# Attention with a hashed mask, then a mixture of experts: the routing's work of a batch on other steps

## The chip, the cores and the metric

The kernel runs on one core of one Trainium2 chip. The time is what the device takes for one execution, in microseconds (us). TensorE (PE, with its weight loads PEld), VectorE (DVE), ScalarE (ACT), GpSimd (POOL) and the DMA queues run side by side, each through its own instructions in order, and wait for each other by semaphores.

## The reference, cut to what matters

Four batches of eight heads attend over 768 positions. A key counts only if its hash bucket (six sign bits of a projection) is the query's. The result, 3072 tokens of 512 values, goes through a mixture of eight experts, of which each token takes the one with the greatest logit.

```python
def _attn_ref(q, k, v, proj):            # (4, 8, 768, 64)
    mask = q_bucket[:, :, :, None] == k_bucket[:, :, None, :]
    scores = np.where(mask, scale * np.matmul(q, k.transpose(0, 1, 3, 2)), -1000000000.0)
    scores = scores - np.max(scores, axis=-1, keepdims=True)
    attn = np.exp(scores)
    attn = attn / (np.sum(attn, axis=-1, keepdims=True) + 1e-09)
    return np.matmul(attn, v)

def _moe_ref(x, w_gate, w_output_gate, w1, w2):    # x (3072, 512)
    logits = x @ w_gate
    e_idx = np.argmax(logits, axis=1)
    ...
    gate_w = probs[np.arange(N), e_idx]
    eom = 1.0 / (1.0 + np.exp(-(x @ w_output_gate)))
    for e in range(E):
        mask = e_idx == e
        h = np.maximum(x[mask] @ w1[e], 0.0)
        out[mask] = gate_w[mask, None] * eom[mask, e, None] * (h @ w2[e])
```

## The kernel before

**The attention loop.** Its unit is a step: one block of 128 queries of one head. Sixteen pairs of heads of twelve steps each make 192 steps, and steps run in groups of two. In step s PE makes the scores (`scores`, L530, into one of two `ps_s` buffers), DVE takes them out with the row minimum (L534, tile `sc`), ACT exponentiates with the row sum (L542), DVE inverts the sums of two steps (L549, L550, tile `rsum`) and POOL multiplies both tiles by them (`normal`, L552), at the start of the group after. Four steps behind its scores a tile is transposed on PE (L563) and copied by ACT to `pts` (L564); behind each group PE multiplies `pts` by the values (L574, into `ps_a`). For the next pair of heads POOL and DVE split the inputs into a rounded part and a rest (L488, L496), PE projects to hash bits (L407, taken out by L410), and SP's DMA queue spreads the parts over the partitions (L505 to L513). A finished pair is copied out (L577, `ot`), transposed in blocks (L586, `xb`) and written to `x_dram` (L593).

**The routing of a batch.** When the four pairs of a batch are done, `routing(b)` makes functions that are put on steps of the batch after. Numbers n count from the start of that batch (step 48(b+1)). `logits` and `tokens` multiply by the gates' weights and turn the result to tokens. `best` finds the maximum and the exponentials. `choose` (L644 to L651) makes the one-hot choice `oneh` and its bf16 copy `ohb`. `gates` (L655 to L663) makes a token's factor. `prefix` (L668 to L673) counts on PE, from `ohb`, how many tokens before it took the same expert; `ranks` (L678 to L683) reads that out and adds to the running `base`. `cols` makes place and columns of the table (`table_cols` L198 to L205, `table_rhs` L211, L215), `hot` the one-hot of the place (L220); `table` sums them on PE (L226) and `entries` adds the sum to `tacc_e` (L229).

**What follows the third batch.** Three batches are routed within the loop; the fourth behind it. At step `late`, behind the third batch's `entries`, `pick` takes the expert with most tokens and loads its number into a register on SP. `early_gather` gathers two blocks of 128 of its tokens from `x_dram` (POOL's queue, L254), `early_turn` transposes them on PE (L266), `early_load` and `early_w1` load the expert's first weights in four pieces and split them on POOL (L175, L178). Behind the loop, the first layer of this expert runs in eight blocks (`fill`) between the fourth batch's routing, and its second weights (w2) are split on POOL.

**What sets the order.** PE, DVE, ACT and POOL run in the order in which the code is written: `plan(step, fn)` puts a function behind that step's own work, and functions of one step run in the order of their planning. The SP queue's order is made by the scheduler. Scratch tiles of the routing have one buffer each (`gp`), as has the PSUM tile `ps_m`.

Of the kernel before, what the change touches and what calls it, by code (L numbers as in the profile page):

```python
# [8 lines left out]
F32 = mybir.dt.float32  # L9
# [10 lines left out]
B, H, S, D = 4, 8, 768, 64  # L20
NB = 6
P = 128
NT = S // P
# [36 lines left out]
def lsh_attention_then_moe(  # L60
# [307 lines left out]
    with ExitStack() as actx:  # L368
# [16 lines left out]
        def plan(step, *fns):  # L385
            at.setdefault(step, []).extend(fns)
# [209 lines left out]
        def routing(b):  # L596
# [56 lines left out]
            def gates():  # L653
                den = gp.tile([P, NT], F32, name="den")
                nc.vector.tensor_reduce(den, st["ex"], AX.X, ALU.add)  # L655
                nc.vector.tensor_tensor(st["en"], st["en"], oh, ALU.mult)
                es = gp.tile([P, NT], F32, name="es")
                nc.vector.tensor_reduce(es, st["en"], AX.X, ALU.add)
                nc.vector.tensor_scalar(den, den, 1e-9, None, ALU.add)
                nc.vector.tensor_scalar(es, es, 1.0, None, ALU.add)  # L660
                nc.vector.reciprocal(den, den)
                nc.vector.reciprocal(es, es)
                nc.vector.tensor_tensor(gate[:, ts], den, es, ALU.mult)  # L663

# [19 lines left out]

            def cols():
                st["oa"], st["pos"] = table_cols(gp, rank[:, ts], NT)
                st["rhs"] = table_rhs(gp, st["oa"], oh, gate[:, ts], toki[:, ts], NT)
# [8 lines left out]
            def entries():  # L696
# [3 lines left out]
                       gates=gates, prefix=prefix, ranks=ranks, cols=cols, hot=hot, table=table, entries=entries)  # L700
# [23 lines left out]
        for b in range(B - 1):  # L724
            r = routing(b)
            for n, fn in ((6, lambda r=r: r["logits"](0, H // 2)), (8, lambda r=r: r["tokens"](0, H // 2)),
                          (10, lambda r=r: r["logits"](1, H // 2)), (12, lambda r=r: r["tokens"](1, H // 2)),
                          (13, r["best"]), (14, r["choose"]), (15, r["gates"]), (16, r["prefix"]), (16, r["ranks"]),
                          (17, r["cols"]), (18, r["hot"]), (20, r["table"]), (20, r["entries"])):
                plan(12 * (H // 2) * (b + 1) + n, fn)  # L730
# [10 lines left out]
        late = 12 * (H // 2) * (B - 1) + 21  # L741
# [77 lines left out]
        for a in range(EARLY):  # L819
            plan(late + 7 + 2 * a, lambda a=a: early_turn(a))  # L820
# [288 lines left out]
```

## Time and profile before

| | |
|---|---|
| median of 3 runs (lowest to highest) | 802.83 us (800.34 to 803.43) |
| the profiled execution, and its span | 799.08 us, 797.4 us |
| PE busy | 772.7 us (97%) |
| DVE busy | 472.4 us (59%) |
| ACT busy | 458.4 us (57%) |
| POOL busy | 383.4 us (48%) |
| DMA, mean rate | 124 GB/s |

The attention loop takes the first 466 us or so of the span, the experts the rest. A busy time is a share over all stages: it says that PE is the engine to watch, and not where it waits. A row of the order of time shows a group of like instructions: start, length, engine, line, operation, tile written and tiles read, shapes, count; in brackets, how long the engine sat idle ahead of it and whose work ended that. Several rows of an engine may overlap a little, since the next instruction starts before the last has drained; the time that one holds its engine is the difference of starts.

### The profile page before, as it was taken

Reading aid. Unit: us, or ns where it says so; the run is one execution under the profiler, and the core shown is the slowest. Engines: PE = TensorE matmul, PEld = TensorE weight load, DVE = VectorE, ACT = ScalarE, POOL = GpSimd, SP = SyncE. Lnnn points to the kernel's source line nnn. Section 1 sums busy time; section 2 is a strip of 40 time slices with the busy share of each in tenths; the row PEclk is TensorE's granted clock in tenths of the full one; section 3 lists DMA queues with packets and bytes.
Section 4 is the critical chain, followed back from the end, with each engine's and each line's share of the span. In section 5 each row is a group of like instructions: output and inputs, shape, how many; then the busy total and the mean of one; then the engine's idle time right before and its main releaser. Section 6 shows DMA issues by size and latency. Waiting matters only on the chain. (4 is left out here: it accounts for less than half of the span.)

```text
span 797.4 us, 13687 instructions
## 1 busy us (share of the span) xinstructions
PE 772.7 (97%) x4674; PEld 606.8 (76%) x4674; DVE 472.4 (59%) x1034; ACT 458.4 (57%) x934; POOL 383.4 (48%) x422
## 2 busy tenths in 40 slices
PE   7999999989999999999999999999999999999997
PEld 4776776666776667676567758888999999988895
DVE  5776666776766867666877537236363635464540
ACT  5877787667777677777677751234152534443331
POOL 6556544335444344543466773273627363745201
PEclk7999999999999999999999999999999999999999
DMA  4553554464464454565374422373444444535501
GB/s 159 127 148 74 113 128 85 104 159 83 105 150 92 98 126 87 125 142 138 63 205 102 119 65 43 120 236 126 143 146 147 154 147 150 171 127 194 198 24 38
DMA packets 84799, 98.88 MB, mean 124 GB/s; under 512 B 57999, under 2 KB 59439, under 8 KB 84720
## 3 DMA queue, kind: packets, MB, share of 16 engines
q1 hardware_dynamic: 79376, 84.58, 40.8%
q0 software_dynamic: 5200, 13.31, 5.1%
q8 instruction: 39, 0.64, 0.3%
q14 instruction: 40, 0.33, 0.1%
q10 hardware_dynamic: 144, 0.02, 0.0%
HBM read 59.49 MB, written 13.11 MB: 91 GB/s over the span
## 5 line engine op out<-in xcount | busy, mean ns | idle before, releaser
L552 POOL TENSOR_SCALAR sc<-sc,rsum 128x768 f32<-128x768 f32 x192 | 180.4, 953 | 224.2 <-DVE rsum L550 116.1
L534 DVE TENSOR_SCALAR_CACHE_REDUCE sc<-ps_s 128x768 f32<-128x768 f32 x192 | 183.2, 956 | 110.7 <-PE ps_s L530 103.6
L564 ACT COPY pts<-ps_t 128x384 f32<-128x384 f32 x384 | 164.2, 481 | 92.3 <-PE ps_t L563 91.8
L542 ACT ACTIVATE sc<-sc,mn 128x768 f32<-128x768 f32 x192 | 181.3, 944 | 28.7 <-DVE sc L534 19.5
L563 PE MATMUL ps_t<-ident,sc 128*128 128x128 f32 x1152 | 158.4, 273 | 6.6 <-POOL sc L552 3.6
L563 PEld LDWEIGHTS ps_t<-ident,sc 128*128 128x128 f32 x1152 | 135.9, 140 | 19.9 <-issue 7.0
L574 PE MATMUL ps_a<-pts,vt 128*64 128x384 f32 x768 | 144.8, 499 | 0.0
L530 PE MATMUL ps_s<-xr,xl 128*128 128x384 f32 x384 | 118.0, 389 | 4.6 <-DVE sc L534 4.5
L530 PEld LDWEIGHTS ps_s<-xr,xl 128*128 128x128 f32 x384 | 58.4, 192 | 75.5 <-issue 31.8
L530 PE MATMUL ps_s<-yr,yl 76*128 76x384 f32 x384 | 101.2, 344 | 1.7 <-POOL yr L439 1.6
L312 PE MATMUL ps_s<-xh,w1h 128*128 128x256 f32 (+7 forms) x288 | 97.7, 339 | 2.8 <-DVE hl L323 2.0
L323 DVE SCALAR_TENSOR_TENSOR hl<-ps_s,hh 128x256 fp32r<-128x256 f32 (+8 forms) x40 | 34.0, 849 | 111.7 <-ACT hh L322 111.7
L312 PE MATMUL ps_s<-xlo,w1h 128*128 128x256 f32 (+7 forms) x288 | 95.9, 333 | 0.0
L312 PE MATMUL ps_s<-xh,w1l 128*128 128x256 f32 (+7 forms) x288 | 95.8, 333 | 0.0
L286 POOL DMA_INDIRECT xq<-x_dram,idx x75 | 83.0, 1107 | 21.6 <-issue 21.3
L329 POOL DMA_INDIRECT out_dram<-yo,sid x29 | 31.4, 1084 | 116.0 <-ACT yo L328 61.8
L574 PEld LDWEIGHTS ps_a<-pts,vt 128*64 128x64 f32 x768 | 46.7, 136 | 50.5 <-issue 48.7
L322 ACT ACTIVATE hh<-ps_s 128x256 fp32r<-128x256 f32 (+8 forms) x40 | 29.1, 727 | 94.6 <-PE ps_s L312 94.6
L530 PEld LDWEIGHTS ps_s<-yr,yl 76*128 76x128 f32 x384 | 71.0, 192 | 2.4 <-POOL yr L439 2.4
L312 PEld LDWEIGHTS ps_s<-xh,w1h 128*128 128x128 f32 x288 | 54.7, 190 | 5.8 <-DVE hl L323 2.5
L312 PEld LDWEIGHTS ps_s<-xh,w1l 128*128 128x128 f32 x288 | 54.7, 190 | 1.1
L312 PEld LDWEIGHTS ps_s<-xlo,w1h 128*128 128x128 f32 x288 | 54.6, 189 | 1.2
(204 smaller groups left out, 1008.1 us busy)
## 6 DMA issues: line engine op xcount, KB each, us to landing
w_raw<-in_w_dram SPq DMA_DIRECT2D x36, 512.0 KB
qk<-in_qkT_dram SPq DMA_DIRECT2D x32, 384.0 KB
xh<-in_w_dram SPq DMA_DIRECT2D x14, 512.0 KB
xlo<-in_w_dram SPq DMA_DIRECT2D x14, 512.0 KB
vt<-in_v_dram SPq DMA_DIRECT2D x16, 384.0 KB
xr<-xl SPq DMA_DIRECT2D x30, 192.0 KB
yr<-xl SPq DMA_DIRECT2D x30, 192.0 KB
xr<-yl SPq DMA_DIRECT2D x30, 192.0 KB
```

Of the source, the lines that this page charges most:

```text
L286: nc.gpsimd.indirect_dma_start(out=xq[:, k * P:(k + 1) * P], out_offset=None, in_=x_dram.rearrange("n (a f) -> (n a) f", a=NB32), in_offse ...
L312: nc.tensor.matmul(ps, l, r, start=first and k == 0, stop=last and k == len(pairs) - 1)
L322: nc.scalar.activation(hh, ph, AF.Relu)
L323: return lambda: nc.vector.scalar_tensor_tensor(hl, ph, 0.0, f32(hh), ALU.max, ALU.subtract)
L329: nc.gpsimd.indirect_dma_start(out=out[:, :], out_offset=bass.IndirectOffsetOnAxis(ap=sid[0:n, r, a:a + 1], axis=0), in_=yo[0:n], in_offse ...
L530: nc.tensor.matmul(ss[:, n, 0:HS], l[0:k, qs], r[0:k, n * HS:(n + 1) * HS], start=first, stop=not first)
L534: nc.vector.tensor_scalar(sc, ss[:, :, 0:HS], MASKED, None, ALU.min, ALU.min, accum_out=mn)
L542: nc.scalar.activation(pr, pr, AF.Exp, bias=mn, scale=-1.0, accum_out=sums[s // GROUP][:, k:k + 1])
L552: nc.gpsimd.tensor_scalar(live[s0 + k], live[s0 + k], rs[:, k:k + 1], 0.0, ALU.mult, ALU.add)
L563: nc.tensor.transpose(tr[:, c], pr[:, (3 * h + c) * P:(3 * h + c + 1) * P], ident)
L564: nc.scalar.copy(pts[:, 3 * h:3 * h + 3, t * P:(t + 1) * P], tr)
L574: nc.tensor.matmul(st["av"][j * D:(j + 1) * D], st["v"][:, j, c], blocks[hb][j][:, c], start=(c == 0), stop=(c == NT - 1))
```

## The change

The functions of `routing` are cut finer. `gates` becomes `gate_sums` (the two sums and the product with the choice) and `gate_values` (the five small operations on them), `cols` becomes `places` and `columns`. `gates` and `cols` themselves remain for the fourth batch, which is routed behind the loop as before. No operation is added or taken away.

For the other three batches the steps are new: choice 14 to 19, prefix and ranks 16 to 20, the gates 15 to 21 and 22, places and columns 17 to 22 and 24, the one-hot 18 to 25, the table 20 to 28 and its addition 20 to 29. Step 24 is the first of the next pair of heads. `late` moves from 21 to 29 steps into the last batch's loop, and with it all that follows the third batch; only the turns of the gathered tokens are planned one step closer to it.

```diff
-            def gates():
-                den = gp.tile([P, NT], F32, name="den")
+            def gate_sums():
+                st["den"] = den = gp.tile([P, NT], F32, name="den")
                 nc.vector.tensor_reduce(den, st["ex"], AX.X, ALU.add)
                 nc.vector.tensor_tensor(st["en"], st["en"], oh, ALU.mult)
-                es = gp.tile([P, NT], F32, name="es")
+                st["es"] = es = gp.tile([P, NT], F32, name="es")
                 nc.vector.tensor_reduce(es, st["en"], AX.X, ALU.add)
+
+            def gate_values():
+                den, es = st["den"], st["es"]
                 nc.vector.tensor_scalar(den, den, 1e-9, None, ALU.add)
...
-            def cols():
+            def places():
                 st["oa"], st["pos"] = table_cols(gp, rank[:, ts], NT)
+
+            def columns():
                 st["rhs"] = table_rhs(gp, st["oa"], oh, gate[:, ts], toki[:, ts], NT)
...
-                          (13, r["best"]), (14, r["choose"]), (15, r["gates"]), (16, r["prefix"]), (16, r["ranks"]),
-                          (17, r["cols"]), (18, r["hot"]), (20, r["table"]), (20, r["entries"])):
+                          (13, r["best"]), (19, r["choose"]), (20, r["prefix"]), (20, r["ranks"]),
+                          (21, r["gate_sums"]), (22, r["gate_values"]), (22, r["places"]), (24, r["columns"]),
+                          (25, r["hot"]), (28, r["table"]), (29, r["entries"])):
                 plan(12 * (H // 2) * (b + 1) + n, fn)
...
-        late = 12 * (H // 2) * (B - 1) + 21
+        late = 12 * (H // 2) * (B - 1) + 29
...
         for a in range(EARLY):
-            plan(late + 7 + 2 * a, lambda a=a: early_turn(a))
+            plan(late + 6 + 2 * a, lambda a=a: early_turn(a))
```

The line numbers of the changed kernel are higher: by 7 from `gate_sums` on, by 15 behind the routing.

On DVE, in the batch that follows batch 0, this stood in a row before, from the projection's bits of step 14 (`bt`) on: the choice, the scores' minimum of step 15, a split of the next pair's inputs, and the gates.

```order
L410 TENSOR_SCALAR bt<-ps_m,pj 128x384
L644 TENSOR_SCALAR eq<-df 128x48
L645 TENSOR_TENSOR eq<-eq,expi 128x48
L647 TENSOR_REDUCE ei<-eq 128x6
L648 TENSOR_TENSOR oneh<-ei,expi 128x48
L651 CAST ohb<-oneh 128x48
L534 TENSOR_SCALAR sc,mn<-ps_s 128x768
L496 SCALAR_TENSOR_TENSOR yl<-qk,pj,xl 128x384
L655 TENSOR_REDUCE den<-ex 128x6
L656 TENSOR_TENSOR en<-en,oneh 128x48
L658 TENSOR_REDUCE es<-en 128x6
L659 TENSOR_SCALAR den<-den 128x6
```

The five rows of the choice stood between the minima of steps 14 and 15, and the gates directly behind step 15's.

On DVE in the changed kernel, from the last split of that pair (step 18) on, to the first rows of the ranks of step 20:

```order
L496 SCALAR_TENSOR_TENSOR yl<-qk,pj,xl 128x384
L534 TENSOR_SCALAR sc,mn<-ps_s 128x768
L644 TENSOR_SCALAR eq<-df 128x48
L645 TENSOR_TENSOR eq<-eq,expi 128x48
L647 TENSOR_REDUCE ei<-eq 128x6
L648 TENSOR_TENSOR oneh<-ei,expi 128x48
L651 CAST ohb<-oneh 128x48
L534 TENSOR_SCALAR sc,mn<-ps_s 128x768
L549 TENSOR_SCALAR rsum<-rsum 128x2
L550 RECIPROCAL rsum<-rsum 128x2
L685 TENSOR_TENSOR off<-ps_m,base 128x48
L686 TENSOR_TENSOR off<-off,oneh 128x48
```

The choice now comes after the splits, between the minima of steps 19 and 20, and the ranks behind step 20's row sums.

On POOL at the end of the loop before, from the rest of the third piece of w1 on to the first of w2 (`x10` are five pairs of normalisations):

```order
L178 TENSOR_TENSOR w1l<-w_raw,w1h 128x1024
L552 TENSOR_SCALAR sc<-sc,rsum 128x768 x2
L175 TENSOR_SCALAR w1h<-w_raw 128x1024
L178 TENSOR_TENSOR w1l<-w_raw,w1h 128x1024
L552 TENSOR_SCALAR sc<-sc,rsum 128x768 x10
L175 TENSOR_SCALAR w2h<-w_raw 128x1024
```

And the same place of the changed kernel:

```order
L178 TENSOR_TENSOR w1l<-w_raw,w1h 128x1024
L552 TENSOR_SCALAR sc<-sc,rsum 128x768 x2
L175 TENSOR_SCALAR w1h<-w_raw 128x1024
L178 TENSOR_TENSOR w1l<-w_raw,w1h 128x1024
L552 TENSOR_SCALAR sc<-sc,rsum 128x768 x2
L175 TENSOR_SCALAR w2h<-w_raw 128x1024
```

One pair of normalisations, the loop's last, now stands behind the fourth piece where five did.

## Rows read from the trace of the kernel before

**Rows 1.** Windows: length, busy PE, PEld, DVE, ACT, POOL, clock, DMA share, GB/s.

```profile
159.17:165.54 6.37, 4.87 (x30) 3.05 (x28) 6.13 (x21) 3.17 (x9) 1.64 (x2) 1.00 0.53 124
165.54:172.45 6.91, 5.92 (x42) 4.45 (x41) 4.53 (x11) 5.78 (x14) 4.56 (x4) 1.00 0.40 84
190.85:195.20 4.35, 4.35 (x30) 3.16 (x28) 3.11 (x8) 3.51 (x9) 1.98 (x3) 1.00 0.40 85
195.20:199.56 4.36, 4.36 (x30) 3.18 (x28) 2.18 (x6) 3.46 (x9) 1.89 (x3) 1.00 0.81 167
199.56:203.94 4.38, 4.38 (x30) 3.16 (x28) 3.23 (x8) 3.43 (x9) 1.81 (x3) 1.00 0.45 119
```

**Rows 2.** Order of time, PE, where the first batch's routing ends.

```profile
161.75 0.62 PE L530 MATMUL ps_s<-xr,xl 128*128 128x384 f32 x2 [0.90 <-DVE sc L534]
...
167.50 0.87 PE L563 MATMUL ps_t<-ident,sc 128*128 128x128 f32 x6 [0.98 <-POOL sc L552]
168.22 1.48 PE L226 MATMUL ps_m<-t_rhs,t_ob 128*128 128x96 f32 x12
169.47 0.59 PE L530 MATMUL ps_s<-xr,xl 128*128 128x384 f32 x2
```

**Rows 3.** Order of time, DVE, the first batch's routing.

```profile
152.09 0.41 DVE L644 TENSOR_SCALAR eq<-df 128x48 f32<-128x48 f32 x1
...
154.42 0.96 DVE L534 TENSOR_SCALAR_CACHE_REDUCE sc<-ps_s 128x768 f32<-128x768 f32 x1
...
155.83 0.19 DVE L655 TENSOR_REDUCE den<-ex 128x6 f32<-128x48 f32 x1
...
156.93 0.55 DVE L577 COPY ot<-ps_a 128x384 f32<-128x384 f32 x1
...
159.06 0.20 DVE L678 TENSOR_TENSOR off<-ps_m,base 128x48 f32<-128x48 f32 x1
...
160.74 0.94 DVE L534 TENSOR_SCALAR_CACHE_REDUCE sc<-ps_s 128x768 f32<-128x768 f32 x1
...
162.61 0.18 DVE L198 TENSOR_TENSOR t_ge<-rank,chki 128x30 f32<-128x30 f32 x1
...
163.21 0.35 DVE L211 TENSOR_TENSOR t_rhs<-oneh,t_oa 128x192 f32<-128x192 f32 x1
...
164.14 0.95 DVE L534 TENSOR_SCALAR_CACHE_REDUCE sc<-ps_s 128x768 f32<-128x768 f32 x1
...
165.81 0.95 DVE L220 TENSOR_TENSOR t_ob<-posi,t_pos 128x768 f32<-128x768 f32 x1
```

**Rows 4.** Order of time, DVE, the odd step's minimum in a quiet window.

```profile
193.56 0.95 DVE L534 TENSOR_SCALAR_CACHE_REDUCE sc<-ps_s 128x768 f32<-128x768 f32 x1
```

**Rows 5.** The tile of gathered tokens (xg), its eight gathers' DMAs.

```profile
DMA to landing us min/median/max: 3.2/3.8/9.6
```

**Rows 6.** Order of time, POOL, the last pairs of heads and the loop's end.

```profile
428.43 1.06 POOL L175 TENSOR_SCALAR w1h<-w_raw 128x1024 fp32r<-128x1024 f32 x1
429.57 2.39 POOL L178 TENSOR_TENSOR w1l<-w_raw,w1h 128x1024 fp32r<-128x1024 f32 x1
432.38 1.79 POOL L552 TENSOR_SCALAR sc<-sc,rsum 128x768 f32<-128x768 f32 x2 [0.42 <-ACT pts L564]
...
459.08 1.80 POOL L552 TENSOR_SCALAR sc<-sc,rsum 128x768 f32<-128x768 f32 x2 [2.85 <-PE ps_s L530]
...
466.95 1.79 POOL L552 TENSOR_SCALAR sc<-sc,rsum 128x768 f32<-128x768 f32 x2 [1.72 <-PE ps_t L563]
```

**Rows 7.** Order of time, PE, the transposes of step 194.

```profile
469.66 0.88 PE L563 MATMUL ps_t<-ident,sc 128*128 128x128 f32 x6
```

**Rows 8.** Order of time, DVE, beside a piece of w1 on POOL.

```profile
430.55 1.43 DVE L549 TENSOR_SCALAR rsum<-rsum 128x2 f32<-128x2 f32 x1
```

**Rows 9.** Order of time, PE, among the experts.

```profile
732.68 0.49 PE L312 MATMUL ps_s<-xh,w1h 128*128 128x368 f32 x1 [1.99 <-DVE hl L323]
```

**Rows 10.** Windows, the stretch behind that wait.

```profile
732.90:736.30 3.40, 3.40 (x12) 3.40 (x12) 3.40 (x4) 3.21 (x4) 1.00 (x1) 0.50 0.49 129
```

More of the change, by code (lines that the diff above doesn't have):

```diff
@@ L663, in gates @@
                 nc.vector.tensor_tensor(gate[:, ts], den, es, ALU.mult)
+            def gates():
+                gate_sums()
+                gate_values()
             def prefix():
@@ L683, in ranks @@
                 nc.vector.tensor_tensor(base, base, tot, ALU.add)
+            def places():
+                st["oa"], st["pos"] = table_cols(gp, rank[:, ts], NT)
+            def columns():
+                st["rhs"] = table_rhs(gp, st["oa"], oh, gate[:, ts], toki[:, ts], NT)
             def cols():
-                st["oa"], st["pos"] = table_cols(gp, rank[:, ts], NT)
-                st["rhs"] = table_rhs(gp, st["oa"], oh, gate[:, ts], toki[:, ts], NT)
+                places()
+                columns()
             def hot():
@@ L699, in routing @@
             fns = dict(logits=logits, tokens=tokens, add_pair=add_pair, best=best, choose=choose,
-                       gates=gates, prefix=prefix, ranks=ranks, cols=cols, hot=hot, table=table, entries=entries)
+                       gates=gates, prefix=prefix, ranks=ranks, cols=cols, hot=hot, table=table, entries=entries,
+                       gate_sums=gate_sums, gate_values=gate_values, places=places, columns=columns)
             return fns
```

## The prediction, made before the changed kernel ran

> **What bounds the kernel now.** I read the granted clock first, then the engines' busy time over pairs of steps, then the order of time on TensorE, VectorE and GpSimd around a batch's routing, and last the end of the attention loop. In the windows of [rows 1] look at PE's busy time against the length of the window: a quiet pair of steps is 4.35 us long and PE is busy for all of it, at full clock. So TensorE sets the pace of the loop, and what another engine does costs nothing while it fits beneath PE. The two windows in which a batch's routing ends are longer, 6.37 and 6.91 us, and PE is busy for only 4.87 and 5.92 of them [rows 1]. What does PE wait for there? In [rows 2] scores wait 0.90 us for a score buffer that VectorE has not emptied (sc L534), and a transpose waits 0.98 us for a normalised tile (sc L552), which hangs on VectorE's row sums. VectorE is busy for 6.13 of 6.37 us there [rows 1]: the bound in this stretch is VectorE's queue, not TensorE. The three batches that are routed inside the loop show the same two lengths within 0.02 us; the fourth is routed behind the loop and isn't moved.
>
> **What the routing costs today.** 6.37 - 4.35 = 2.02 us in the first window. In the second, 6.91 - 4.35 = 2.56 us, of which the table's matmuls are PE's own work: they run from 168.22 to the next scores at 169.47, 1.25 us [rows 2], so 1.31 us are lost. Together 3.33 us a batch, 10.0 us for three. The prefix matmuls and the logits lie in other pairs of steps and cost PE the same wherever they stand.
>
> **Part 1: the work of VectorE is spread.** Nothing is removed: the same instructions run per batch. From [rows 3], by the difference of starts: the choice takes 152.09 to 154.42, 2.33 us; the eight gate operations 155.83 to 156.93, 1.10; the ranks 159.06 to 160.74, 1.68; the places 162.61 to 163.21, 0.60; the columns 163.21 to 164.14, 0.93; the one-hot 0.95. Before, choice, gates, ranks, places, columns and one-hot stand in steps 14 to 18 of the pair, and these are also the steps in which the next pair's splits (L496) run. After, they stand in steps 19 to 25.
> I add each share to VectorE's busy time in the quiet windows of the same place in a pair [rows 1], which stand there in the order of steps 18, 20 and 22 (that of 24 repeats the one of 20, two minima and a row sum, 2.18):
> - steps 18 and 19: 3.11 + 2.33 (choice) = 5.44 in 4.35, so VectorE falls 1.1 us behind.
> - steps 20 and 21: 2.18 + 1.68 (ranks) + 1.10 (I put all eight gate operations here, which is the worse case) = 4.96: 0.6 more, 1.7 behind.
> - steps 22 and 23: 3.23 + 0.60 = 3.83: it gains 0.5.
> - steps 24 and 25: 2.18 + 0.93 + 0.95 = 4.06: it gains 0.3 more. After that the table's sum (step 28) gives PE 1.25 us of its own, and its addition on VectorE is a single operation.
> How far may VectorE fall behind before PE feels it? In a quiet pair the odd step's minimum begins at 193.56 [rows 4], 1.64 us ahead of the next window's start at 195.20. Before PE's first wait it began at 160.74 [rows 3], 1.57 us behind the window's start at 159.17: 3.2 us late, and PE waited 0.90. So the cover is about 2.3 us. A lag of 1.7 stays beneath it, with 0.6 to spare. If that cover were gone, the wait of 0.90 would come back and after it the one of 0.98. One wait is new in its place: PE's prefix (step 20) needs the choice of step 19. The choice starts after step 19's minimum, 2.7 + 0.95 = 3.65 us into its window (193.56 less the window's start of 190.85, and the length of that row [rows 4]), and ends 5.4 to 6.0 us in; PE comes to the prefix behind six transposes of the next window, later than 5.4. I bound this wait by 0 and 0.5 us a batch and take 0.1, since the dear choice was measured beside a busy GpSimd throughout and this one only in part: 0.3 us for three batches. **Gain of part 1: 10.0 - 0.3 = 9.7 us** (bounds 8.5 and 10.0 while the cover holds).
>
> **Part 2: the last batch's followers move eight steps.** The table ends at step 173 instead of 164, so the pick of the first expert, its gathers, turns, weight loads and weight splits follow; the turns come four steps behind the gather where it was five.
> - On SP the pick's register load now stands between the two heads' spreads of the last pair. Both are waiting there for VectorE's splits of steps 172 to 174, so I cost it at nothing; the loads of w1 come behind the spreads now instead of ahead. They land with some two steps in hand before their splits. If that cover is gone, TensorE waits at the end for w1.
> - The gathers land 3.2 to 9.6 us after issue, median 3.8 [rows 5]. Four steps are two windows, 8.7 us. I take nothing; one landing of 9.6 would cost PE about 2 to 3 us, since PE's queue is in order.
> - GpSimd: each w1 piece costs 1.06 + 2.39 = 3.45 us [rows 6]. The pieces stood in steps 174 to 183, with four pairs of steps behind them to recover. Now the last two stand at steps 188 and 191. In program order GpSimd has, from 459.08 on, a pair of normalisations (1.80), a piece (3.45), a pair (1.8), a piece (3.45): it is free for the last pair of normalisations at 469.6, which started at 466.95 before [rows 6]. The first of the two is done some 0.9 us later (half of the 1.79 of both), at 470.5; PE wants it at 469.66 [rows 7]. So PE waits about 0.9 us, and the second tile is about as late: **1.0 us lost**, bounds 0 (a piece that starts sooner) and 2.7 (the whole lateness of GpSimd).
> A piece also holds up VectorE. An operation on 128x2 elements took 1.43 us, from 430.55 to 431.98 [rows 8], and GpSimd's subtraction, from 429.57 on, ended at 431.96 [rows 6]; the normalisation that needs this row sum began 0.42 us behind it, at 432.38 [rows 6]. If both late pieces hit their row sum so, the tail is dearer by 2 x 0.42 = 0.8 us. Whether they do hangs on a few tenths of a microsecond, so I leave it to a rival. The Trainium skill has a rule for this (SBUF — State Buffer, "SBUF: two separate sides"): VectorE in a two-port mode and GpSimd share a port pair as an exclusive lock, and whoever starts second is held for the whole instruction. By that rule the tail would cost 1.8 us and the sum would be 0.8 smaller in gain; the trace agrees with the lock here, to 0.02 us.
> Behind the loop, the w2 pieces on GpSimd start up to 2.7 us later. Their products are wanted only after the eight blocks of the first layer and the routing of the last batch, so I cost this at nothing.
>
> **Sum.** -9.7 + 1.0 = -8.7 us. Against the profiled execution (799.08 us, span 797.4) this is 790.4. The runs' median is 802.83, 3.75 above the profiled one; the edit acts on stretches that don't depend on what separates runs, so I subtract from the median: **794.1 us**, 1.1% faster.
>
> **The rivals.**
> 1. *The tail is dearer.* Two late pieces with locked row sums (0.8), or a wait of PE that drops its clock. At 732.68 PE had waited 1.99 us, and the 3.40 us behind it ran at half the clock, 1.2 GHz [rows 9, 10], which costs half of that, 1.7 us. Against it: the waits of 0.90 and 0.98 left the clock at 1.00 in both windows [rows 1], and mine in the tail is 1.0. Time: 794.1 + 0.8 + 1.7 = 796.6.
> 2. *The wait only moves.* The lag of 1.7 us grows past 2.3, by a dear choice, a busier GpSimd or the prefix wait, and PE waits 2 us a batch at steps 21 to 23 instead of 3.33. The gain is 3 x 1.33 - 1.0 = 3.0: 799.8, within 0.5%. For it: only 0.6 us of cover is left. Against it: my lag puts all gates in the worst place.
> 3. *Slower: VectorE's queue overflows twice a batch.* If choice and ranks (steps 19 to 21) pass the cover and columns and one-hot (24, 25) pass it again before it has recovered, PE pays the 3.33 us of today at both: 3.33 x 3 = 10.0 us more than now and 1.0 in the tail, 813.8. It decides at a lag above 2.3 us in both places. Against it: steps 22 to 25 leave VectorE 0.8 us to recover, by the sums above.
> 4. *The order isn't the cause.* The waits come from the SP queue's spreads or from something that moves along with the routing. Then nothing is gained and the tail is paid: 803.8. Against it: PE's waits in [rows 2] end with VectorE's and GpSimd's tiles.
>
> **How the numbers follow.** The forecast 0.62, rival 1 0.20, rival 2 0.11, rival 3 0.03, rival 4 0.04. A measurement of this kernel can tell about 0.5% from no change, 4 us: faster means under 798.8. Forecast and rival 1 are faster, and a fifth of rival 2; rest of rival 2 and rival 4 are the same. Faster 0.84, same 0.13, slower 0.03. The range runs from the forecast without a tail cost and without the wait at 732.68 with its half clock (1.99 + 1.7 = 3.7), 794.1 - 1.0 - 3.7 = 789.4, rounded to 790.0, since both at once is unlikely, to between rival 1 and rival 2, 798.5.
>
> **What would show it right or wrong.** After: the three long windows are gone. The pair of steps 20, 21 is longer than 4.35 only by the prefix, and that of step 28 by some 1.25 us of table; PE's waits for sc L534 and sc L552 in the middle of the loop vanish; VectorE never runs without a gap for more than two pairs of steps. At the end GpSimd's last w1 piece stands directly ahead of the last normalisations and a transpose of step 194 waits about 1 us. Wrong: PE waits for ohb at the prefix, waits for sc in steps 21 to 26, waits for the gathered rows or w1 before the first expert, or a half clock behind the tail.

## The result, and the profile after

| | before | after |
|---|---|---|
| median, runs on the first chip | 802.83 us (7 runs, 800.34 to 806.62) | 797.50 us (7 runs, 793.06 to 797.87) |
| the profiled execution, and its span | 799.08 us, 797.4 us | 795.53 us, 793.8 us |
| last scores matmul of the loop begins at | 463.87 us | 454.77 us |
| first block of the first layer begins at | 473.07 us | 465.28 us |

The ratio of the runs is 0.9935, 95% interval 0.9915 to 0.9955: 5.3 us less, 0.65%, where 8.7 us less were forecast. The loop gives what was forecast almost whole (9.1 us), and what follows it takes much of that back.

The page, the line of the engines, and TensorE's waits (total, times, longest):

```profile
PE 771.9 (97%) x4674; PEld 607.3 (77%) x4674; DVE 479.1 (60%) x1034; ACT 458.6 (58%) x934; POOL 381.2 (48%) x422
```

```profile
PE ps_s L312 <- DVE hl L323: 4.0, 3, 2.5
PE ps_s L530 <- DVE sc L534: 1.8, 1, 1.8
PE ps_t L563 <- ACT pts L564: 1.6, 4, 0.4
PE ps_t L563 <- POOL sc L552: 1.5, 2, 1.2
...
PE ps_s L312 <- ACT w1h L177: 1.2, 1, 1.2
```

The one wait left for `sc` L534 stands at the loop's start, as in every kernel here; those of [rows 2] are gone. Gone with them is a wait that [rows 2] leave out. In the first long window of each batch of the kernel before, TensorE waited a third time, for a buffer of the transposes, behind an exponential for which ScalarE had stood idle for 1.57 us:

```profile
163.33 0.84 PE L563 MATMUL ps_t<-ident,sc 128*128 128x128 f32 x6 [0.60 <-ACT pts L564]
```

In its place the changed kernel has three waits of 0.42 us for `pts` in another window. New are two for `sc` L552 at the loop's end, and two more for `hl`, on which the first layer's blocks hang.

**The loop.** The windows of the changed kernel that answer to [rows 1]: the pairs of steps 18, 20, 22, 24 and 28 of the first batch's routing.

```profile
158.57:162.93 4.36, 4.36 (x31) 3.16 (x29) 3.76 (x10) 3.52 (x9) 1.99 (x3) 1.00 0.40 84
162.93:167.55 4.62, 4.62 (x38) 3.42 (x36) 4.08 (x17) 3.20 (x9) 1.90 (x3) 1.00 0.79 162
167.55:171.90 4.35, 4.35 (x30) 3.15 (x28) 3.82 (x14) 3.34 (x8) 1.80 (x2) 1.00 0.45 126
171.90:176.89 4.99, 4.57 (x31) 3.10 (x29) 4.89 (x14) 3.45 (x8) 1.97 (x2) 1.00 0.68 192
182.24:187.94 5.70, 5.70 (x43) 4.51 (x41) 4.28 (x11) 3.71 (x10) 2.75 (x3) 1.00 0.25 53
```

PE is busy for the whole of every one but that of step 24: 4.57 of 4.99 us. The pair of step 20 is longer by its prefix matmuls (0.27 us), that of step 28 by the table (1.35). A batch's four pairs of heads take 113.38 us, 116.18 before: 2.80 us a batch.

What is the 0.42 us in step 24's window? VectorE between the minima of steps 22 and 23, ScalarE behind it, and PE:

```profile
169.87 0.17 DVE L663 TENSOR_SCALAR es<-es 128x6 f32<-128x6 f32 x1
...
170.29 0.71 DVE L666 TENSOR_TENSOR gate<-den,es 128x6 f32<-128x6 f32 x1
170.92 0.18 DVE L198 TENSOR_TENSOR t_ge<-rank,chki 128x30 f32<-128x30 f32 x1
171.13 0.77 DVE L201 TENSOR_TENSOR t_oa<-t_ge 128x24 f32<-128x24 f32 x1
...
172.13 0.96 DVE L534 TENSOR_SCALAR_CACHE_REDUCE sc<-ps_s 128x768 f32<-128x768 f32 x1
```

```profile
173.13 0.94 ACT L542 ACTIVATE sc<-sc,mn 128x768 f32<-128x768 f32 x1 [1.66 <-DVE sc L534]
173.97 0.19 ACT L542 ACTIVATION_READ_ACCUMULATOR sc<-sc,mn 128x1 f32 x1
174.07 0.84 ACT L564 COPY pts<-ps_t 128x384 f32<-128x384 f32 x2
```

```profile
174.67 0.85 PE L563 MATMUL ps_t<-ident,sc 128*128 128x128 f32 x6 [0.42 <-ACT pts L564]
```

Gate values (here L662 to L666, three lines on from the kernel before) and places stand on one step. The odd minimum begins at 172.13, 0.23 us behind the next window's start at 171.90; in a quiet pair it begins 1.64 ahead of it ([rows 4] with [rows 1]), so VectorE is 1.87 us late. The scores' buffers bear that. But ScalarE stands idle for 1.66 us in front of this exponential, and its copies out of `ps_t` stand behind it in its queue, so the transposes wait for a buffer.

**The loop's end.** GpSimd's order, answering to [rows 6], and the transposes of [rows 7]:

```profile
455.67 1.79 POOL L552 TENSOR_SCALAR sc<-sc,rsum 128x768 f32<-128x768 f32 x2 [0.42 <-DVE rsum L550]
457.43 1.05 POOL L175 TENSOR_SCALAR w1h<-w_raw 128x1024 fp32r<-128x1024 f32 x1
458.56 2.36 POOL L178 TENSOR_TENSOR w1l<-w_raw,w1h 128x1024 fp32r<-128x1024 f32 x1
460.88 1.81 POOL L552 TENSOR_SCALAR sc<-sc,rsum 128x768 f32<-128x768 f32 x2
```

```profile
461.86 0.87 PE L563 MATMUL ps_t<-ident,sc 128*128 128x128 f32 x6 [1.22 <-POOL sc L552]
463.02 0.89 PE L563 MATMUL ps_t<-ident,sc 128*128 128x128 f32 x6 [0.29 <-POOL sc L552]
```

The fourth piece of w1 stands directly ahead of the last normalisations. From the last scores to the first block the kernel before takes 9.20 us, the changed one 10.51: 1.3 us.

**Among the first layer's blocks.** GpSimd's last piece of w2, VectorE and PE:

```profile
475.41 1.05 POOL L175 TENSOR_SCALAR w2h<-w_raw 128x1024 fp32r<-128x1024 f32 x1 [1.59 <-DMA w_raw<-in_w_dram]
476.55 2.44 POOL L178 TENSOR_TENSOR w2l<-w_raw,w2h 128x1024 fp32r<-128x1024 f32 x1
```

```profile
475.78 0.74 DVE L648 TENSOR_TENSOR oneh<-ei,expi 128x48 f32<-128x48 f32 x1
...
477.14 0.38 DVE L323 SCALAR_TENSOR_TENSOR hl<-ps_s,hh 128x256 fp32r<-128x256 f32 x1
477.45 0.18 DVE L655 TENSOR_REDUCE den<-ex 128x6 f32<-128x48 f32 x1
477.56 1.50 DVE L656 TENSOR_TENSOR en<-en,oneh 128x48 f32<-128x48 f32 x1
479.09 0.20 DVE L658 TENSOR_REDUCE es<-en 128x6 f32<-128x48 f32 x1
```

```profile
477.58 0.39 PE L312 MATMUL ps_s<-xh,w1h 128*128 128x256 f32 x1 [0.38 <-DVE hl L323]
...
480.31 0.39 PE L312 MATMUL ps_s<-xh,w1h 128*128 128x256 f32 x1 [1.09 <-DVE hl L323]
```

The fourth batch's choice and gates run here. L648 takes 0.74 us beside GpSimd's cast and L656 1.50 beside its subtraction; in this kernel's loop both took about 0.2 us. L656 ends at 479.06, the subtraction at 478.99. `hl` stands behind them in VectorE's queue, and PE needs the score buffer that `hl` empties. The lead over the kernel before (how much sooner the same matmul begins) falls by 1.6 us here.

**A stop that isn't the order's.** This trace holds one more loss, at the second expert's start: ScalarE's `yo` (L328) stands behind 8.22 us of idle time and the casts of the weights behind it, and PE waits.

```profile
526.84 0.69 ACT L328 ACTIVATE yo<-ps_m,tacc 128x512 f32<-128x512 f32 x1 [8.22 <-issue]
527.42 1.03 ACT L177 CAST w1h<-xh 128x1024 fp32r<-128x1024 f32 x1
```

```profile
528.51 0.48 PE L312 MATMUL ps_s<-xh,w1h 128*128 128x464 f32 x1 [1.21 <-ACT w1h L177]
```

A second trace of the same program (`repeat`, below) hasn't got it. The first is 0.7 us ahead of the second in front of this place and 2.1 us behind it afterwards, so the stop is worth some 2.8 us.

### The profile page after: what moved, and what is told of

It reads as the page before. It is cut to its first block, busy times and chain, and to the rows that moved or that the text cites. A ratio compares the mean times of both kernels' runs of the same rounds, so it can differ in the third digit from the quotient of the medians.

```text
span 793.8 us, 13687 instructions
## 1 busy us (share of the span) xinstructions
PE 771.9 (97%) x4674; PEld 607.3 (77%) x4674; DVE 479.1 (60%) x1034; ACT 458.6 (58%) x934; POOL 381.2 (48%) x422
## 5 line engine op out<-in xcount | busy, mean ns | idle before, releaser
L552 POOL TENSOR_SCALAR sc<-sc,rsum 128x768 f32<-128x768 f32 x192 | 179.0, 944 | 219.2 <-DVE rsum L550 88.6
L534 DVE TENSOR_SCALAR_CACHE_REDUCE sc<-ps_s 128x768 f32<-128x768 f32 x192 | 183.3, 955 | 98.1 <-PE ps_s L530 90.1
L574 PE MATMUL ps_a<-pts,vt 128*64 128x384 f32 x768 | 144.8, 499 | 0.0
L574 PEld LDWEIGHTS ps_a<-pts,vt 128*64 128x64 f32 x768 | 46.6, 136 | 50.5 <-issue 47.7
```

The costliest lines, as they stand in the source:

```text
L534: nc.vector.tensor_scalar(sc, ss[:, :, 0:HS], MASKED, None, ALU.min, ALU.min, accum_out=mn)
L552: nc.gpsimd.tensor_scalar(live[s0 + k], live[s0 + k], rs[:, k:k + 1], 0.0, ALU.mult, ALU.add)
L574: nc.tensor.matmul(st["av"][j * D:(j + 1) * D], st["v"][:, j, c], blocks[hb][j][:, c], start=(c == 0), stop=(c == NT - 1))
```

## The experiments

Three sets and one single run, each on a chip of its own with runs of the kernel before beside it. The chips differ (the kernel before takes 798.2, 802.6, 797.6 and 801.4 us), so I give the ratio to the runs beside it and set lengths of windows side by side.

### The same kernel again, and its two halves

**repeat**: the changed kernel, no edit.

> The changed kernel again, unaltered. The first trace of it has a stop at expert 1's start that the kernel before hasn't: TensorE waits 2.3 us between 528 and 531 us, because ScalarE casts the weights late after 8.2 us of idle time. Theory 'the order makes it': the stop comes again within 0.5 us, the profiled execution again takes 795 to 796 us, the ratio is 0.993. Rival 'an accident of that execution': the stop is under 0.5 us, and the profiled execution takes 792 to 793.5 us; the ratio over many runs would still be 0.993, since the runs without a profile hold it.

Ratio 0.993 (0.9912 to 0.9949), 792.44 against 798.20 us. The stop is gone: `yo` comes 5.6 us sooner.

```profile
521.21 0.69 ACT L328 ACTIVATE yo<-ps_m,tacc 128x512 f32<-128x512 f32 x1 [1.94 <-issue]
```

The loop, the tail's waits (1.22 and 0.29) and the waits among the blocks (0.43 and 1.23) are as in the first trace. So the ratio is the order's, and the stop doesn't come with the order each time.

**late_only**: the old steps for the routing, the new ones for what follows the third batch.

```diff
-                          (13, r["best"]), (19, r["choose"]), (20, r["prefix"]), (20, r["ranks"]),
-                          (21, r["gate_sums"]), (22, r["gate_values"]), (22, r["places"]), (24, r["columns"]),
-                          (25, r["hot"]), (28, r["table"]), (29, r["entries"])):
+                          (13, r["best"]), (14, r["choose"]), (15, r["gates"]), (16, r["prefix"]), (16, r["ranks"]),
+                          (17, r["cols"]), (18, r["hot"]), (20, r["table"]), (20, r["entries"])):
```

> The routing stands on its old steps (13 to 20) and only the first expert's choice, gather, turns and weights stand where the changed kernel has them (from step 173 in place of 165). Theory 'the second part is a loss': three routing stops of 3.3 us stay as in the kernel before, TensorE waits 1.2 to 1.5 us on the last transposes and 1.5 us more among the fills (VectorE's operations of 0.2 us taking 0.7 and 1.5 beside GpSimd's last w2 piece), so 805.7 us, and 808.7 if the stop at expert 1's start (3.0) also comes from it. Rival 'moving the first expert is free': 802.8 us, within 0.5 of the kernel before.

Ratio 1.004 (1.0027 to 1.0054), 801.76 us: 3.2 us slower by the ratio, 2.9 expected without the stop. The second part alone is a loss. The long windows stand as before (4.80, 6.37, 6.91 us), and three waits of PE come among the blocks: 0.60 and 0.44 us for `hl`, and 1.33 for the fourth batch's choice (`ohb`). The operation that is held up is another one here, the choice's first, from 484.10 until 0.05 us after the end of GpSimd's last subtraction (483.87 to 486.25):

```profile
484.10 2.20 DVE L644 TENSOR_SCALAR eq<-df 128x48 f32<-128x48 f32 x1
```

**two_batches**: the new steps for batches 0 and 1, the old ones for batch 2 and all that follows it.

```diff
-                          (13, r["best"]), (19, r["choose"]), (20, r["prefix"]), (20, r["ranks"]),
...
+                          (13, r["best"])) + (((19, r["choose"]), (20, r["prefix"]), (20, r["ranks"]),
...
+                          (25, r["hot"]), (28, r["table"]), (29, r["entries"])) if b < B - 2 else
+                          ((14, r["choose"]), (15, r["gates"]), (16, r["prefix"]), (16, r["ranks"]),
+                          (17, r["cols"]), (18, r["hot"]), (20, r["table"]), (20, r["entries"]))):
...
-        late = 12 * (H // 2) * (B - 1) + 29
+        late = 12 * (H // 2) * (B - 1) + 21
...
-            plan(late + 6 + 2 * a, lambda a=a: early_turn(a))
+            plan(late + 7 + 2 * a, lambda a=a: early_turn(a))
```

> The new steps for the routing of batches 0 and 1 alone; batch 2 keeps the old steps, and the first expert's choice, gather, turns and weights stand where the kernel before has them. Theory 'each batch gives 2.8 us, the second part takes some back': two batches give 5.6 us and no cost behind them, so 797.2 us, no slower than the changed kernel with three batches; the groups at 20 to 28 of batches 0 and 1 last as in the changed kernel, and the last transposes don't wait. Rival 'the stops of the end are paid by any kernel that reaches it sooner': the loop ends 6 us sooner and the gathers and fills hand 2 to 3 of it back, 800 us.

Ratio 0.9924 (0.9909 to 0.9939), 791.92 us: 6.1 us less than before. 113.37 us for each of the two batches, no wait for GpSimd on the last transposes. Two batches moved are worth as much as three: what the third gives, its followers take.

**weights_early**: of the followers, the choice of the expert and its weights 6 steps earlier.

```diff
-        plan(late, pick)
+        early_at = late - 6
+        plan(early_at, pick)
...
-            plan(late + 9 + 3 * cc, lambda cc=cc: early_w1(cc))
-            plan(late + (3 + cc if cc < 2 else 3 + 3 * cc), lambda cc=cc: early_load(cc))
+            plan(early_at + 9 + 3 * cc, lambda cc=cc: early_w1(cc))
+            plan(early_at + (3 + cc if cc < 2 else 3 + 3 * cc), lambda cc=cc: early_load(cc))
```

> The changed kernel with the first expert's choice on step 167 (its ranks are ready on 165) and the loads and splits of its w1 counted from there, 6 steps ahead of where the changed kernel has them; gather and turns stay. Theory 'the delayed weight pieces on GpSimd cost the tail': the 1.2 us wait on the last transposes goes (-1.2), the last w2 piece ends some 6 steps sooner and no VectorE operation among the fills takes over 0.7 us (-1.2), so 795.1 us, and 792 if the stop at expert 1's start goes with it. Rival 'the tail's waits come from elsewhere': 797.5 us, as the changed kernel. Second rival: the choice's six VectorE operations on step 167 make the scores wait up to 1 us there: 796 us.

Ratio 0.9905 (0.989 to 0.992), 790.59 us: 7.6 less than before, as the first theory has it. The wait on the last transposes is gone, and so are both among the blocks (one of 0.67 us for `eq` is there, as in the kernel before). One window of the last batch (steps 182 and 183), behind two splits in neighbouring groups, now takes 5.2 us in place of 4.35.

### Dividing or moving?

**moved_whole**: the old undivided pattern, five steps later.

```diff
+            for n, fn in (...
+                          (13, r["best"]), (19, r["choose"]), (20, r["gates"]), (21, r["prefix"]), (21, r["ranks"]),
+                          (22, r["cols"]), (23, r["hot"]), (25, r["table"]), (25, r["entries"])):
```

> The routing is not divided: its five pieces stand in the old pattern, 5 steps later (choice 19, gates 20, prefix and ranks 21, table columns 22, one-hot 23, table and entries 25); the first expert's work stays where the changed kernel has it. The places 19 to 25 are free of the next pair's low parts (L496, steps 15 to 18), which stand among the old places. Theory 'the place gains it': most of the 2.8 us per batch comes, 1.9 or more, and the kernel takes 5.7 us less than before at the least 3 us of that. Rival 'the dividing gains it': a bunch of five pieces is too long for the 2.3 us of cover wherever it stands, 0.9 us or less per batch comes, and the kernel is within 1 us of the one before or up to 3 us slower.

Ratio 0.9956 (0.9941 to 0.9971). A batch takes 114.43 us: 1.74 of the 2.80 us. One long window is left, and in it waits for the score buffer and for `pts`:

```profile
171.92:179.28 7.36, 6.13 (x43) 4.50 (x41) 5.83 (x14) 4.75 (x11) 3.33 (x4) 1.00 0.64 154
```

```profile
174.23 0.62 PE L530 MATMUL ps_s<-xr,xl 128*128 128x384 f32 x2 [0.68 <-DVE sc L534]
175.75 0.84 PE L563 MATMUL ps_t<-ident,sc 128*128 128x128 f32 x6 [0.55 <-ACT pts L564]
```

**divided_old**: the changed kernel's pieces and distances, five steps earlier.

```diff
+                          (13, r["best"]), (14, r["choose"]), (15, r["prefix"]), (15, r["ranks"]),
+                          (16, r["gate_sums"]), (17, r["gate_values"]), (17, r["places"]), (19, r["columns"]),
+                          (20, r["hot"]), (23, r["table"]), (24, r["entries"])):
```

> The changed kernel's divided pieces in the changed kernel's pattern, all 5 steps earlier (choice on its old step 14, one-hot 20, table 23, entries 24), so that the first three lie among the next pair's low parts; the first expert's work stays where the changed kernel has it. Theory 'the place gains it': 0.9 us or less of the 2.8 per batch comes, so at most 1 us faster than the kernel before, or up to 3 slower (the second part's cost of 3.2 stays). Rival 'the dividing gains it': 1.9 us or more per batch, and 3 to 6 us faster than before.

Ratio 0.9978 (0.9965 to 0.9992). A batch takes 114.57 us: 1.60 of the 2.80. What is left is a wait that no other kernel has in the loop, PE's prefix for the choice:

```profile
154.41 0.20 PE L675 MATMUL ps_m<-ohb,tri 128*128 128x48 bf16 x1 [1.56 <-DVE ohb L651]
```

Neither theory holds as it stood: either half of the change alone brings about 60%, and together they bring 2.80, less than the sum. Both lighten the same queue, which would explain that; it isn't shown. Nor do these two runs part place from pattern cleanly. Five steps are an odd number, and steps run in groups of two: the choice of step 19 and the prefix of step 20 lie in two groups, with a group's products (L574, 1.44 us by the starts) between them on PE, while those of steps 14 and 15 lie in one group, and its products come behind the prefix. The wait of 1.56 us may be that, or the dearer choice among the splits (2.4 us from L644 to L651's end, 1.6 in the changed kernel). A shift by an even number of steps, or a prefix two steps behind the choice, wasn't tried.

**places_23**: `places` one step later, the rest as changed.

```diff
-                          (21, r["gate_sums"]), (22, r["gate_values"]), (22, r["places"]), (24, r["columns"]),
+                          (21, r["gate_sums"]), (22, r["gate_values"]), (23, r["places"]), (24, r["columns"]),
```

> The changed kernel with the places (L198 to L205) on step 23 in place of 22, where they stand behind the gate values. In the changed kernel the two take 2.4 us of VectorE between two scores, and TensorE waits 0.42 us on the transposes behind them in each of three batches (the 4.98 us group). Theory 'these two are one piece too many on a step': the wait goes, the group takes 4.5 to 4.6 us, 1.2 us less than the changed kernel in all, 7 us less than before. Rival 'the wait belongs to the piece on step 24': the group stays at 5.0 us or grows, 5.7 us less than before.

Ratio 0.9915 (0.9897 to 0.9933): 6.8 us less than before, 7 expected. A batch takes 112.75 us, 0.62 less than changed, and the window of step 24 is full:

```profile
171.97:176.34 4.37, 4.37 (x30) 3.17 (x29) 4.17 (x13) 3.56 (x8) 1.83 (x2) 1.00 1.11 277
```

```profile
170.99 0.94 DVE L534 TENSOR_SCALAR_CACHE_REDUCE sc<-ps_s 128x768 f32<-128x768 f32 x1
...
172.54 0.18 DVE L201 TENSOR_TENSOR t_oa<-t_ge 128x24 f32<-128x24 f32 x1
```

The odd minimum begins at 170.99 in place of 172.13. And L201, which took 0.77 us beside a normalisation of GpSimd, takes 0.18 here.

### The followers, placed

**best1**: as weights_early, but from `late - 8`, so that choice of the expert and splits of w1 are back on their old steps (165; 174, 177, 180, 183), and with `places` on 23.

```diff
-        plan(late, pick)
+        early_at = late - 8
+        plan(early_at, pick)
```

> The changed kernel with the places on step 23 and the first expert's choice, loads and splits of w1 back on their old steps (choice 165, right behind the ranks; splits 174, 177, 180, 183); gather and turns stay where the changed kernel has them. Theory 'the loop's gain without the late weights': 1.3 us of tail and 2.0 us of waits among the fills of the changed kernel are gone, and 1.2 us of the transposes' waits, so 9 to 10.5 us less than before, ratio 0.987 to 0.989. Rival 'what is taken off one place is paid at the next': the choice delays scores on step 165, and the splits on 174 to 180 delay normalisations there by 0.8 us, as the group of 5.2 us in the kernel with the choice on 167: 7.6 us less than before.

Ratio 0.9917 (0.9902 to 0.9932): nothing over places_23. The rival is right, by a mechanism that neither had named so: the gather's two issues (step 175) now stand behind a split, and the normalisations behind both.

```profile
418.43 2.38 POOL L178 TENSOR_TENSOR w1l<-w_raw,w1h 128x1024 fp32r<-128x1024 f32 x1
420.98 1.18 POOL L254 DMA_INDIRECT xg<-x_dram,gid  x1 [0.18 <-DVE rsum L549]
422.47 0.97 POOL L254 DMA_INDIRECT xg<-x_dram,gid  x1 [0.30 <-DVE ot L577]
423.48 1.79 POOL L552 TENSOR_SCALAR sc<-sc,rsum 128x768 f32<-128x768 f32 x2
```

```profile
424.44 0.88 PE L563 MATMUL ps_t<-ident,sc 128*128 128x128 f32 x6 [1.87 <-POOL sc L552]
```

**best2**: the splits on 176, 180, 184 and 188.

```diff
-                          (21, r["gate_sums"]), (22, r["gate_values"]), (22, r["places"]), (24, r["columns"]),
+                          (21, r["gate_sums"]), (22, r["gate_values"]), (23, r["places"]), (24, r["columns"]),
...
-        plan(late, pick)
+        plan(late - 8, pick)
...
-            plan(late + 9 + 3 * cc, lambda cc=cc: early_w1(cc))
-            plan(late + (3 + cc if cc < 2 else 3 + 3 * cc), lambda cc=cc: early_load(cc))
+            plan((176, 180, 184, 188)[cc], lambda cc=cc: early_w1(cc))
+            plan((168, 169, 176, 180)[cc], lambda cc=cc: early_load(cc))
```

> The changed kernel with the places on step 23, the first expert's choice back on step 165, and the splits of w1 on 176, 180, 184 and 188, so that no two stand in neighbouring groups of two steps and none ahead of the gather on 175 (the kernel with splits from 174 lost 2.5 us there: the gather's two issues came after a split, the normalisation 2 us late, and TensorE waited 1.9 us on it). Theory 'GpSimd holds one piece of 3.4 us in two groups beside its normalisations': last batch's groups sum to 109.6 to 110.2 us as with the late splits, the tail's wait is under 0.5 us, the fills have no new wait, and the kernel is 9 to 10 us under the one before (ratio 0.9875 to 0.989). Rival 'some wait stays wherever the pieces stand': 7 to 8 us less than before.

Ratio 0.9883 (0.9865 to 0.9901), 788.80 against 797.61 us, the fastest here: 9.3 us less than before. Its last batch, up to the scores of step 190, takes 110.08 us (110.27 in the changed kernel's first trace, 109.65 in places_23), and no transpose waits for GpSimd at the loop's end. GpSimd's last subtraction for w2 ends ahead of the fourth batch's gates, which take their 0.2 us again:

```profile
470.57 2.39 POOL L178 TENSOR_TENSOR w2l<-w_raw,w2h 128x1024 fp32r<-128x1024 f32 x1
```

```profile
475.22 0.19 DVE L656 TENSOR_TENSOR en<-en,oneh 128x48 f32<-128x48 f32 x1
```

**best4**: the same with splits on 176, 179, 182 and 185 (loads 168, 169, 176, 179).

> As the kernel with splits on 176, 180, 184, 188, but with them on 176, 179, 182 and 185, the steps of the kernel with the choice on 167, where a group of the last batch took 5.2 us in place of 4.35. Theory 'neighbouring pieces cost 0.8 us': 0.5 to 0.9 us slower than the spread-out splits, 8.3 to 9.3 us less than before. Rival 'the earlier end of the pieces is worth more': as fast or faster than the spread-out ones.

Ratio 0.9892 (0.9874 to 0.991); the intervals overlap, but its last batch takes 110.61 us against 110.08, a window of 5.21 among them: two pieces in neighbouring groups cost 0.5 us.

### The stop

**before_again** and **before_third**: the kernel before, no edit, on two more chips.

> The kernel before, unaltered, for one more trace. Five of ten traces so far (the first of the changed kernel and the four of the second set) have a stop of 2.3 to 3.0 us at expert 1's start, the other five have none; the chip of the second set also runs the kernel before 4.4 us slower than the other. Theory 'the stop belongs to the chip or the execution, not to the order': where the kernels beside this one show it, this one does too, with ScalarE's casts of the weights 2 us or more late behind idle time that no release explains. Rival 'the changed order brings it': this one has none, whatever its neighbours show.

> The kernel before, unaltered, on whatever chip is free. The stop at expert 1's start was seen on the two chips on which the kernel before takes 802.5 to 802.8 us, and not on the two on which it takes 797.6 to 798.2. Theory 'the stop belongs to the chip': if this chip runs it in 801 us or more, the trace has the stop (2 us or more of TensorE's time between 520 and 535 us that the other two traces of this kernel haven't); if it takes 799 or less, it has none. Rival 'the changed order brings it': no stop at either time.

The first decides nothing: no stop in it (`yo` at 526.98) and none in its neighbours, best2 and best4. The second came on a chip that runs this kernel in 801.4 us (9 runs, 799.4 to 805.9), and it has the stop, as all four traces of the second set have:

```profile
530.66 0.69 ACT L328 ACTIVATE yo<-ps_m,tacc 128x512 f32<-128x512 f32 x1 [4.82 <-issue]
```

`yo` is 3.7 us later than in before_again, and TensorE loses 2.0 us between 519 and 541 us, by small stops put down to issue (0.45, 0.31, 0.26) and a later gather (0.82), not by the weights as in the first trace of the changed kernel. Only about 1.1 us of that fall before 535 us, where the theory asked for 2. So the late `yo` is in the kernel before too, and what it costs TensorE differs. It goes with the chip or the execution, though not with the chip alone: on the first chip the kernel before hasn't got it. The six traces with it also lack about a thousand of the 11,200 semaphore records, all but some fifty of them after 505 us and nearly all landings of DMAs; a wait put down to issue there may be one for a DMA whose record is missing. What makes ScalarE late stays open.

## Why the prediction was right or wrong

The forecast was 8.7 us, 9.7 of the loop less 1.0 of the tail; 5.3 and 5.8 were measured, inside the range. The 797.5 us lie next to rival 1's 796.6, and that is luck: most of what is missing was lost in a place that neither the forecast nor a rival named. By two traces without the stop, before_again and repeat, the lead of the changed kernel is 9.0 us at the loop's last scores, 7.7 at the first block, 8.5 at the fourth and 6.5 behind the waits there, 5.8 once the gathered rows have landed (0.7 on their landings; between the two traces of the changed kernel these differ by 0.5). From 8.7 to 5.8 that is 0.7 less in the loop, 0.5 more at its end, 2.0 lost among the blocks and 0.7 on the landings.

- **What bounds the kernel: right.** VectorE's queue made the long windows. Both waits of [rows 2] are gone, and rival 4 falls. But the reading was not complete: the third wait of these windows, 0.60 us for `pts`, isn't in it.
- **The gain of part 1: right, 9.0 for 9.7.** A batch gave 2.80 us, not 3.33 less 0.1: the window of step 24 took 0.64 more than the quiet 4.35 (0.42 of it a wait; places_23 wins back 0.62), the table 1.35 for 1.25, and 0.2 came back ahead of [rows 1], in a window of 4.81 us that I hadn't counted. The prefix waited for nothing; 0.1 was allowed. Three batches make 8.4; the other 0.55 comes with the followers, which leave the loop in part (late_only has it alone: 113.06 us for the last batch's loop, 113.61 in before_again). I put it down to the pieces of w1; no run moves them alone from the kernel before.
- **The lag: wrong in place, and right in size by luck.** I put the worst at the pair of step 20, 1.7 us, and let it fall to 1.2 at step 22. Measured by the odd minimum it is 0.4 at step 20 (166.33 for a window that ends at 167.55) and 1.87 at step 22, where gate values and places stand. The choice took 1.6 us (L644 from 162.13 on, L651 until 163.77), not 2.33, and the ranks 1.1, not 1.68. All gates on step 20, put in as the worse case, was the better one: on step 22 the sum had 0.60 us of places, and gate values and places took 2.3 (169.81 to 172.13). VectorE was busy for 3.76, 4.08, 3.82 and 4.89 us in the four windows where 5.44, 4.96, 3.83 and 4.06 were worked out.
- **The cover: the step that failed inside part 1.** 2.3 us was read off the score buffers. The lag of 1.87 stayed beneath it, and no score waited. But a second cover ends sooner: ScalarE's queue, in which a late exponential holds up the copies that free `ps_t`. 1.87 of lag gave 0.42 of wait, so that cover is about 1.45 us, an estimate from this one window. I had read one path from VectorE to PE where there are two, and the second stood in the trace before, as the wait of 0.60 us at 163.33. places_23, with the odd minimum 1.14 us sooner, takes the wait away.
- **The tail: right in mechanism, 1.3 for 1.0.** The last piece stands ahead of the last normalisations as forecast; 1.22 us of wait where 0.9 was worked out. The 0.42 us of idle time of [rows 6] stands ahead of the normalisations of 455.67, so the third piece did hit its row sum (L549 took 1.49 us, from 453.78 on); 0.9 and 0.42 are nearly the 1.22. The fourth held up the last row sum too (1.03 us), at no cost, since its normalisations stand behind the piece in any case. The clock stayed full; rival 1 came in part by its first term.
- **"Behind the loop the w2 pieces cost nothing": the step that failed.** I asked when w2's products are wanted, and not what the pieces do to others while they run. Shifted by the late w1, and the last by 1.6 us of waiting for its load, they reach the fourth batch's choice and gates, and cost 2.0 us (repeat); weights_early, with the weights sooner, loses none of it. The Trainium skill (SBUF — State Buffer, "SBUF: two separate sides") lets VectorE's operations with two SBUF inputs, or in a two-port mode, wait for the whole of a GpSimd instruction that holds the shared ports. The trace agrees closely: within one subtraction of 2.44 us, `hl` with an input in PSUM (0.38) and a reduction (0.18) pass, and the product of two SBUF tiles (1.50) waits until 0.07 us after its end. So the rule that I had cited for the tail was the rule for this place.
- **What I left out in the other direction.** The kernel before waits 0.8 us among the blocks for the fourth batch's choice (`eq`, L644). The changed kernel doesn't: its blocks begin 1.3 us later behind the same routing. In the traces, each kernel that waits on its last transposes is without this wait, and each that doesn't has 0.5 to 0.8 us of it (best2 0.67). So up to 0.8 of the tail's 1.3 is only paid sooner, and the locks among the blocks are the greatest part of the shortfall.
- **SP and the gathers at nothing: right.** No trace of the changed kernel has a wait in the loop for w1 or for the rows gathered on step 175. The time in hand was less than the 8.7 us worked out, though: 6.5 from the gather's issue (419.7) to its first turn (426.24).
- **The half clock.** Behind the wait of [rows 9], 2.50 us here, the granted clock is 0.50 again for 3.4 us, as in [rows 10]:

```profile
730.50:733.90 3.40, 3.40 (x13) 3.40 (x12) 3.40 (x4) 2.13 (x3) 1.00 (x1) 0.50 0.64 200
```

In before_again and weights_early the wait is 1.63 and 2.10 us, and the clock stays at 1.00. The loss is up to 1.7 us of one execution, and belongs to no kernel here.

## What to carry to other kernels

Work that is spread off a busy queue takes its followers with it: here the last batch's gain was paid out again by weight pieces on GpSimd that arrived among other work; placing them anew, with `places` one step later, made 5.3 us into 9.3 (by ratios of two chips). Cost a piece on GpSimd by what it does to VectorE's small operations beside it, such as a product of two SBUF tiles or a row sum, not only by when its result is wanted. And before a lag is called covered, follow every queue between the late engine and the one that sets the pace: the shortest cover counts, and it may lie on an engine that is itself idle.

## What the runs showed of the hardware that I had not expected

- How much the neighbour matters to a small operation: 128x48 elements took 0.19 us or 1.50 (L656), 128x24 elements 0.18 or 0.77 (L201), and a row sum of 128x2 elements 0.17 or, in best1, 2.72 us, beside a pair of normalisations (from 423.48) and the cast behind them on GpSimd, and until the cast's end:

```profile
423.58 2.72 DVE L549 TENSOR_SCALAR rsum<-rsum 128x2 f32<-128x2 f32 x1
```

- Chips differ by 0.6% on the same program (797.6 to 802.8 us for the kernel before), and one stop at one place can be 2.0 to 2.8 us of a time.
- The clock's drop behind a wait of about 2 us is not settled by the wait's length: 1.99 and 2.50 us (the kernel before, the changed one) were followed by 3.4 us at half the clock, 2.10 and 2.28 (weights_early, places_23) by none.
